# Attention and a two-matmul MoE block with Mish: three batches in one hand-ordered stream, one table set for Exp and Ln, Mish in one batched pass

## The chip, the cores and the metric

The kernel runs on one core of a Trainium2 chip. The metric is device time of one execution in microseconds (us), the median of several runs; shorter is better. A core has five engines that work side by side, each on its own queue: TensorE (PE, matmuls into PSUM, with weight loads called PEld), VectorE (DVE), ScalarE (ACT, activation functions from loaded tables), GpSimd (POOL) and SyncE (SP, here only a DMA queue).

## The reference, cut to what matters

```python
# q, k, v: (8 batches, 12 heads, 448 tokens, 64), scaled by 0.1
scores = (q @ k.T) / 8
m = max(scores); e = exp(scores - m)
attn = e / (sum(e) + exp(-m))          # softmax "off by one"
x = (attn @ v), heads side by side     # (3584 tokens, 768)
h = x @ w_in                           # 768 -> 2048
g = h * tanh(softplus(h))              # Mish
out = g @ w_out                        # 2048 -> 768
```

Without the maximum, the softmax is exp(s) / (sum(exp(s)) + 1), and both kernels compute it so: 1/(1+sum) is exp(-Ln(1+sum)).

## The kernel before

It works in two phases. All of attention comes first, two heads (a "pair") at a time, 48 pairs; the tokens' activations then stay in SBUF. The MoE phase follows in chunks of 512 tokens. The tile framework orders the instructions.

```python
# attention, for each of the two heads of a pair: four key tiles of 128 (the last padded)
for t in range(NSK):
    nc.tensor.matmul(sc_ps, lhsT=kT_bf[:, c0 + t*SKP : c0 + (t+1)*SKP], rhs=qT_bf, ...)  # zero-padded k
    nc.scalar.activation(out=eT_bf[:, t, :], in_=sc_ps, func=AF.Exp, scale=SCALE)        # L249
...                                       # av_ps: 64 rows of values, row 64 is the sum
nc.scalar.activation(out=dln[...], in_=av_ps[D:D+1, :], func=AF.Ln, bias=1.0)            # L277
nc.scalar.activation(out=rp[0:33, :], in_=dln, func=AF.Exp, scale=-1.0)                  # L127
nc.tensor.matmul(bc_ps, lhsT=blk_ones, rhs=rp, ...)     # spread the reciprocal over 64 rows
nc.vector.tensor_mul(xT_sb[...], av_keep[h_off][0:D, :], bc_sb[...])

# MoE, for each 128 x 512 tile of h (112 of them): Mish as h - h * 2/((1+e^h)^2 + 1)
nc.scalar.activation(out=u_sb, in_=h_ps, func=AF.Exp)                                    # L323
nc.scalar.activation(out=v_sb, in_=u_sb, func=AF.Square, bias=1.0)                       # L324
nc.scalar.activation(out=t_sb, in_=v_sb, func=AF.Ln, scale=0.5, bias=half_bias)          # L325
nc.scalar.activation(out=r_sb, in_=t_sb, func=AF.Exp, scale=-1.0)                        # L328
nc.vector.tensor_mul(p_sb, h_ps, r_sb)
nc.vector.tensor_sub(gT_bf[:, ff, :], h_ps, p_sb)
```

## Time and profile before

| | before |
|---|---|
| time, median | 1082.11 us (three runs; 1082.96 with a fourth) |
| ACT busy | 982.9 us of 1084.0 (91%) |
| PE busy (modelled) | 681.1 us (63%) |
| table loads on ACT | 341 of 1283 ns, 437 us |
| granted TensorE clock | 0.802 mean |

From the page of the kernel before: busy time of the engines, the granted clock of PE over 40 equal slices of the span (in tenths), and the engines' shares of the chain that ended last (a q marks an engine's sequencer).

```profile
PE 681.1 (63%) x2768; PEld 310.3 (29%) x2768; DVE 376.6 (35%) x962; ACT 982.9 (91%) x1345; POOL 60.4 (6%) x102
PEclk9766776778787766767877888888888888889889
ACT 62%; PE 21%; issue 13%; DVE 2%; DMA 1%; SPq 0%; ACTq 0%; POOL 0%; DVEq 0%
```

ACT is nearly always busy and holds most of the chain. What it is busy with is seen in its groups of instructions (line, engine, operation, count | busy us, mean ns of one | idle before):

```profile
L325 ACT ACT_TABLE_LOAD x112 | 143.7, 1283 | 2.0
L323 ACT ACT_TABLE_LOAD x81 | 103.9, 1283 | 1.4
L277 ACT ACT_TABLE_LOAD x58 | 74.4, 1283 | 1.0
L249 ACT ACT_TABLE_LOAD x46 | 59.0, 1283 | 15.2 <-DMA q_f_175<-in_q_dram 14.4
...
```

Exp and Ln alternate, and each change from one to the other is one load: in the MoE phase every Ln (L325, 112 tiles) and most of the Exps of L323 (81 of 112) need one. With 31 and 13 more before two further Exps, 341 in all, the loads take 44% of ACT's busy time (437 of 983 us) and compute nothing.

PE's own pace shows in two windows (start:end, length, then busy us and count of PE, PEld, DVE, ACT, POOL; PE clock, DMA share, GB/s). The first is ordinary MoE work, the second the last 34 us, where only the second matmul is left:

```profile
900.00:1000.00 100.00, 65.51 (x272) 29.58 (x272) 29.91 (x45) 98.77 (x123) 0.00 (x0) 0.86 0.06 23
1050.00:1084.00 34.00, 30.36 (x186) 18.06 (x184) 8.02 (x12) 12.71 (x20) 0.00 (x0) 0.98 0.18 70
```

With ACT out of the way PE gets a clock of 0.98. The timeline there has 16 matmuls of 512 columns plus 16 of 256 every 5.20 us: 12,288 columns, 2.36 per ns.

### The profile page before, as it was taken

The numbers are of one execution on the slowest core, as the hardware profiler recorded it, in microseconds if no ns is written. First come the engines' busy times: TensorE is split into PE (matmuls) and PEld (weight loads), VectorE is DVE, ScalarE is ACT, GpSimd is POOL, SyncE is SP. The second block draws the span as 40 slices with busy tenths as digits, with TensorE's granted clock in tenths as the row PEclk, the third lists the DMA queues.
The fourth block names the chain that finished last, engine by engine and source line by source line (L and its number), as shares of the span: only waits on it lengthen the run. The fifth ranks groups of instructions, "written<-read, shape, count | busy, mean of one in ns | idle before, by whom it ended". The sixth has DMA issues, their size and how long they took to land.

```text
span 1084.0 us, 9227 instructions
## 1 busy us (share of the span) xinstructions
PE 681.1 (63%) x2768; PEld 310.3 (29%) x2768; DVE 376.6 (35%) x962; ACT 982.9 (91%) x1345; POOL 60.4 (6%) x102
## 2 busy tenths in 40 slices
PE   3665666666666655656556656666677676676578
PEld 1322322332222222222222222232233232232235
DVE  5334443445444333322323323323223223223222
ACT  3888988888898889989999999999999999999992
POOL 2111111111111100000000000000000000000000
PEclk9766776778787766767877888888888888889889
DMA  9334444444433322200000000000000000000002
GB/s 241 90 78 111 111 120 119 108 104 118 106 77 77 74 54 58 48 1 1 0 1 29 0 30 0 15 15 29 15 15 30 15 15 30 15 15 29 15 15 88
DMA packets 143282, 57.24 MB, mean 53 GB/s; under 512 B 136064, under 2 KB 136064, under 8 KB 143232
## 3 DMA queue, kind: packets, MB, share of 16 engines
q1 hardware_dynamic: 139200, 44.07, 16.3%
q10 hardware_dynamic: 4032, 12.58, 3.7%
q8 instruction: 22, 0.36, 0.1%
q14 instruction: 28, 0.23, 0.1%
HBM read 45.61 MB, written 11.01 MB: 52 GB/s over the span
## 4 chain that ended last, share of the span: by engine, by line
ACT 62%; PE 21%; issue 13%; DVE 2%; DMA 1%; SPq 0%; ACTq 0%; POOL 0%; DVEq 0%
ACT L323 9%; PE sc_ps L242 9%; ACT t_sb L325 7%; PE av_ps L268 7%; ACT eT_bf L249 6%; ACT u_sb L323 6%; ACT L249 5%; ACT L277 5%; ACT v_sb L324 5%; ACT r_sb L328 5%; ACT L325 3%; ACT L328 3%; ACT dln_pair_71 L277 2%; ACT dln_pair_72 L277 2%; PE o_ps L340 2%
## 5 line engine op out<-in xcount | busy, mean ns | idle before, releaser
L311 PE MATMUL h_ps<-xT_sb,w_in_sb 128*128 128x512 bf16 x672 | 211.6, 464 | 202.5 <-DVE gT_bf L331 202.4
L249 ACT ACTIVATE eT_bf<-sc_ps 128x448 bf16<-128x448 f32 x384 | 200.0, 539 | 54.6 <-PE sc_ps L242 52.5
L329 DVE TENSOR_TENSOR p_sb<-h_ps,r_sb 128x512 f32<-128x512 f32 x112 | 77.5, 692 | 392.9 <-ACT r_sb L328 392.9
L268 PE MATMUL av_ps<-eT_bf,v_aug 128*65 128x448 bf16 x384 | 183.2, 495 | 17.6 <-ACT eT_bf L249 16.8
L311 PEld LDWEIGHTS <-w_in_sb 128*128 128x128 bf16 x672 | 74.4, 111 | 322.7 <-issue 278.2
L325 ACT ACT_TABLE_LOAD x112 | 143.7, 1283 | 2.0
L340 PE MATMUL o_ps<-w_out_sb,gT_bf 128*128 128x512 bf16 x448 | 134.7, 434 | 1.2 <-DVE o_sb L357 1.2
L242 PE MATMUL sc_ps<-qT_bf,kT_pad_75 128*128 128x448 bf16 x192 | 95.7, 502 | 60.7 <-ACT eT_bf L249 56.5
L242 PE MATMUL sc_ps<-qT_bf,kT_pad_76 128*128 128x448 bf16 x192 | 92.3, 482 | 64.5 <-ACT eT_bf L249 63.7
L268 PEld LDWEIGHTS <-v_aug 128*65 128x65 bf16 x384 | 59.2, 154 | 172.8 <-issue 166.7
L323 ACT ACT_TABLE_LOAD x81 | 103.9, 1283 | 1.4
L137 DVE CAST bc_sb<-bc_ps 128x448 bf16<-128x448 f32 x48 | 30.0, 625 | 186.1 <-PE bc_ps L135 182.6
L325 ACT ACTIVATE t_sb<-v_sb,half_bias 128x512 f32<-128x512 f32 x112 | 80.8, 722 | 1.3
L331 DVE TENSOR_TENSOR gT_bf<-h_ps,p_sb 128x512 bf16<-128x512 f32 x112 | 77.4, 691 | 4.0
L277 ACT ACT_TABLE_LOAD x58 | 74.4, 1283 | 1.0
L249 ACT ACT_TABLE_LOAD x46 | 59.0, 1283 | 15.2 <-DMA q_f_175<-in_q_dram 14.4
L328 ACT ACTIVATE r_sb<-t_sb 128x512 f32<-128x512 f32 x112 | 69.8, 624 | 0.3
L324 ACT ACTIVATE v_sb<-u_sb 128x512 f32<-128x512 f32 x112 | 69.5, 620 | 0.5
L348 PE MATMUL o_ps<-w_out_sb,gT_bf 128*128 128x256 bf16 x448 | 69.7, 296 | 0.0
L340 PEld LDWEIGHTS <-gT_bf 128*128 128x128 bf16 x448 | 49.9, 111 | 68.7 <-issue 33.2
L323 ACT ACTIVATE u_sb<-h_ps 128x512 f32<-128x512 f32 x112 | 66.5, 593 | 0.9
L141 DVE TENSOR_TENSOR xT_sb<-av_ps,bc_sb 64x448 bf16<-64x448 f32 x96 | 59.1, 616 | 5.2
(331 smaller groups left out, 590.6 us busy)
## 6 DMA issues: line engine op xcount, KB each, us to landing
out_dram<-o_sb SPq DMA_DIRECT2D x28, 384.0 KB, 2.3
stage<-in_moe_w_in_dram ACTq DMA_DIRECT2D x12, 512.0 KB, 4.5
stage<-in_moe_w_out_dram ACTq DMA_DIRECT2D x16, 384.0 KB, 3.2
q_f_108<-in_q_dram SPq DMA_DIRECT2D x2, 112.0 KB, 6.1
k_f_109<-in_k_dram SPq DMA_DIRECT2D x2, 112.0 KB, 6.6
q_f_175<-in_q_dram SPq DMA_DIRECT2D x2, 112.0 KB, 4.9
k_f_176<-in_k_dram SPq DMA_DIRECT2D x2, 112.0 KB, 5.6
q_f_261<-in_q_dram SPq DMA_DIRECT2D x2, 112.0 KB, 4.0
```

Source lines behind the costliest of these rows:

```text
L242: nc.tensor.matmul(sc_ps, lhsT=kT_bf[:, c0 + t * SKP : c0 + (t + 1) * SKP], rhs=qT_bf, start=True, stop=True,)
L249: nc.scalar.activation(out=eT_bf[:, t, :], in_=sc_ps, func=AF.Exp, scale=SCALE)
L268: nc.tensor.matmul(av_ps, lhsT=v_augs[h_off][:, t, :], rhs=eT_bfs[h_off][:, t, :], start=(t == 0), stop=(t == NSK - 1),)
L277: nc.scalar.activation(out=dln[h_off * 32 : h_off * 32 + 1, :], in_=av_ps[D : D + 1, :], func=AF.Ln, bias=1.0,)
L311: nc.tensor.matmul(h_ps, lhsT=w_in_sb[:, dm, ff * 128 : (ff + 1) * 128], rhs=xT_sb[:, dm, t0 : t0 + TOK_CHUNK], start=(dm == 0), stop=(dm ...
L323: nc.scalar.activation(out=u_sb, in_=h_ps, func=AF.Exp)
L324: nc.scalar.activation(out=v_sb, in_=u_sb, func=AF.Square, bias=1.0)
L325: nc.scalar.activation(out=t_sb, in_=v_sb, func=AF.Ln, scale=0.5, bias=half_bias)
L328: nc.scalar.activation(out=r_sb, in_=t_sb, func=AF.Exp, scale=-1.0)
L329: nc.vector.tensor_mul(p_sb, h_ps, r_sb)
L331: nc.vector.tensor_sub(gT_bf[:, ff, :], h_ps, p_sb)
L340: nc.tensor.matmul(o1_ps, lhsT=gT_bf[:, ff, ts * 128 : (ts + 1) * 128], rhs=w_out_sb[:, ff, 0:N1], start=(ff == 0), stop=(ff == FF_T - 1),)
```

## The change

The intent: take ACT off the critical path and keep PE busy without a break.

- One table set that holds Exp and Ln is loaded by hand; Mish is one table pass, run in a batch for 16 tiles at once.
- Attention of batch p, the first matmul of batch p-1 and the second matmul of batch p-2 run in one stream whose order is written by hand. A slot is one head pair plus a few "units" of MoE work (one h tile, or half of one output tile).
- Keys are cut into 384 (three tiles of 128) plus a tail of 64. The score matmuls of the two heads use the two 64-row halves of PE side by side, and so do the tails of attention times v.
- 64 ones columns stand beside v, so the sum of a head arrives in 64 rows at once; the matmul that spread the reciprocal is gone.
- The weights are cast to bf16 by the DMA itself, issued by GpSimd.

The diff, cut to its core (some lines joined, comments added):

```diff
-        sc_ps, lhsT=kT_bf[:, c0 + t * SKP : c0 + (t + 1) * SKP], rhs=qT_bf,      # 8 a pair
-        nc.scalar.activation(out=eT_bf[:, t, :], in_=sc_ps, func=AF.Exp, scale=SCALE)
+            for h in range(2):
+                r = slice(h * D, h * D + D)
+                nc.tensor.matmul(sp[:, h, 0:S], lhsT=qk[r, S + t * 128 : S + (t + 1) * 128],
+                                 rhs=qk[r, 0:S], start=True, stop=True)
+            nc.scalar.activation(out=e[:, 2 * t : 2 * t + 2, :], in_=sp[:, :, 0:S], func=AF.Exp, ...)
 [...]
+            nc.scalar.activation(out=ln[r, :], in_=av[h][o, 0:S], func=AF.Ln, bias=1.0)
+        nc.scalar.activation(out=rc, in_=ln, func=AF.Exp, scale=-1.0)
 [...]
-                nc.scalar.activation(out=u_sb, in_=h_ps, func=AF.Exp)
-                nc.scalar.activation(out=v_sb, in_=u_sb, func=AF.Square, bias=1.0)
-                nc.scalar.activation(out=t_sb, in_=v_sb, func=AF.Ln, scale=0.5, bias=half_bias)
-                nc.scalar.activation(out=r_sb, in_=t_sb, func=AF.Exp, scale=-1.0)
-                nc.vector.tensor_mul(p_sb, h_ps, r_sb)
-                    nc.vector.tensor_sub(gT_bf[:, ff, :], h_ps, p_sb)
+    def mish(b):
+        for i in range(4):
+            nc.scalar.activation(out=gm[:, f, :], in_=h_sb[:, f, 0:MAIN], func=AF.Mish)
+        nc.scalar.activation(out=gt[:, :, o : o + TAIL], in_=h_sb[:, :, MAIN:S], func=AF.Mish)
+        nc.scalar.preload_act_table_set("natural_log_exp_and_others")
 [...]
+        def slot(j, units):
+            if j + 3 < J: load(j + 3)
+            if j + 2 < J: do_cast(j + 2)
+            rest = max(0, len(units) - 2)
+            scores(j, 0); take(1); transposes(j + 1); take(1)
+            attend(j - 1); scores(j, 1); take((rest + 1) // 2)
+            normalize(j - 1); take(len(units))
+        for p in range(B):
+            m1 = mm1_units(p - 1) if p >= 1 else []
+            m2 = mm2_units(p - 2) if p >= 2 else []
+            for i in range(NPAIR):           # slot 0: 4 of m2; slots 1 to 4: 4 of m1; slot 5: rest of m2
+                ...
+                if i == 4 and p >= 1:
+                    mish(p - 1)              # under it: 8 units of m2
```

## The prediction

> **What bounds the kernel now.** ScalarE (ACT). The page gives it 982.9 us of the 1084.0 us span; VectorE 376.6, TensorE (PE) 681.1 of modelled busy time. The chain that ended last is 62% ACT. The groups of instructions show why: 341 ACT_TABLE_LOADs of 1283 ns, 437 us in all, because Exp and Ln alternate. In the MoE stage (from about 496 us) each 128x512 tile costs four ACT passes (593, 620, 722, 624 ns) and two loads: ACT is 98-99% busy there, 86-90% in attention.
>
> PE is starved: in the windows from 50 to 1050 us its granted clock is 0.67 to 0.86. Only the last 34 us, pure second matmul, run at 0.98: there 16 matmuls of 512 columns plus 16 of 256 take 5.20 us, 2.36 columns per ns.
>
> **What the change does to ACT.** The table set with both Exp and Ln is loaded by hand, so loads fall to about 17 (22 us). The Trainium skill ("ScalarE: Activation LUTs", Table sets) says that one set holds both; this trace shows no such set in use. Per head pair, 8 Exps of 448 (539 ns, about 460 back to back) become three of 896 (about 0.91 us) and one of 448, plus two Ln and one Exp of 448: 4.8 us, 230 us in all. Mish becomes one pass from SBUF, about 7 us a batch. ACT total: about 310 us (estimate from the durations above). It leaves the critical path.
>
> **VectorE:** transpose copies, two 64x448 multiplies a pair (616 ns), 112 h copies (about 0.6 us), 56 output copies: about 200 us, not binding.
>
> **PE becomes the bound.** Columns streamed: mm1 344,064, mm2 344,064, scores 150,528, attention times v 172,032, transposes 43,008: 1,053,696, or 446 us at 2.36 columns per ns. If the K=64 score pairs and the v tails, in different row halves, run concurrently, 86,000 columns vanish: 409 us. The skill ("TensorEngine Tiling (Array Packing)", Key Properties) says that changing the tiling mode drains PE, so I count half of that gain.
>
> **Sum by stage** (estimates):
> - start and batch 0, attention alone, competing with 12.6 MB of weights: 60 us
> - batch 1: 52 us, its Mish (10 us with two loads) covered by no second matmul
> - six steady batches: 51-56 us of PE plus 2-4 us of waits, 56 each: 336 us
> - last attention, mm1 of batch 7 with direct Mish, mm2 of batches 6 and 7, last store: 67 us
>
> Predicted: 515 us, 475 to 565 for 8 in 10. Faster by over 2%: 0.98; same 0.01; slower 0.01.
>
> **What would show it.** Right: about 17 table loads; ACT below 65% of the span; PE clock above 0.93 from about 60 us on; PE busy above 85%; chain mostly PE; steady period about 56 us. The score matmuls of a pair start within tens of ns of each other if they run concurrently, about 190 ns apart if not. Wrong: ACT still over 80% (loads inserted anyway, or slow Mish passes); clock still at 0.8 in the dense part (then 600 us or more); PE idle at the PSUM pools of two buffers (transposes and av share one), over 1 us a slot; the first matmul of batch 1 waiting for w_in beyond 70 us.
>
> **What would make it wrong.** Weight casts in the DMA issued by GpSimd may arrive late or be starved; a stall per slot of 1 us is worth 48 us; the in-order ACT queue may put one pair's Ln behind another's Exps.

## The result, and the profile after

The changed kernel takes 548.13 us (544.7 to 548.82) against 1082.96, and gives a correct result. The ratio is 0.5052, 95% interval 0.5032 to 0.5071. Ratios here are the mean time of one kernel's fast runs over that of the other's in the same rounds, so they differ a little from the ratio of the quoted medians. A second set of runs, the control of the last experiments, gave 547.44 us:

> The changed kernel unchanged, as the control beside the three that follow on the same chip: 548 us within 3, ratio to the kernel before 0.503 to 0.507.

From the page of the changed kernel, the same three lines:

```profile
PE 483.3 (88%) x2768; PEld 234.0 (43%) x2768; DVE 206.3 (38%) x414; ACT 297.9 (55%) x419; POOL 130.2 (24%) x400
PEclk9999869986999899999999899999999999989999
PE 82%; ACT 6%; DMA 6%; SPq 3%; DVE 1%; issue 1%; POOL 0%; POOLq 0%
```

ACT has fallen from 91% to 55% of a span half as long, and the chain is now PE. Of the table loads, 16 are left (these 14, one at the start and one at the Mish of the last batch), from its groups of instructions:

```profile
L233 ACT ACT_TABLE_LOAD x7 | 9.0, 1283 | 0.1
L235 ACT ACT_TABLE_LOAD x7 | 9.0, 1283 | 0.1
L233 ACT ACTIVATE gm<-h_sb 128x1536 bf16<-128x1536 f32 x28 | 39.2, 1470 | 0.1
```

Mish runs at one table pass's price: 1536 columns in 1.47 us. The span cut by stage, with the boundaries at the first score matmul of slots 6 and 12 and at the last pair's attention (windows, columns as above):

```profile
0.00:70.70 70.70, 34.84 (x138) 11.16 (x139) 15.21 (x37) 27.01 (x40) 31.28 (x91) 0.95 0.85 186
70.70:126.50 55.80, 43.97 (x234) 18.85 (x234) 22.77 (x47) 36.88 (x51) 15.47 (x49) 0.84 0.28 76
126.50:481.50 355.00, 346.32 (x2069) 171.73 (x2068) 158.59 (x315) 221.34 (x295) 83.45 (x260) 0.98 0.30 85
481.50:546.40 64.90, 58.17 (x329) 32.22 (x327) 9.72 (x18) 12.67 (x37) 0.00 (x0) 0.96 0.14 49
```

| stage | predicted | measured |
|---|---|---|
| start and batch 0 | 60 | 70.7 |
| batch 1 | 52 | 55.8 |
| six steady batches | 336 (56 each) | 355.0 (59.2 each) |
| last attention and MoE tail | 67 | 64.9 |

(The records of the clock begin at 60.2 us and read 1.00 before that, so the 0.95 of the first line is too high: the matmuls of batch 0 run at half speed, as experiment 10 shows.) The first and the third stage hold nearly all of the surplus. For the third, here is one steady slot of PE (timeline: start us, duration, engine, line, operation, operands, count):

```profile
255.81 0.55 PE L149 MATMUL s_ps<-qk 64*128 64x448 bf16 x4
256.29 1.31 PE L205 MATMUL h_ps<-xT,w_in_sb 128*128 128x448 bf16 x6
257.44 0.33 PE L125 MATMUL tr_ps<-ident,qmb 128*128 128x128 bf16 x3
257.70 0.20 PE L129 MATMUL tr_ps<-ident,qtb 64*128 64x64 bf16 x1
257.83 0.34 PE L125 MATMUL tr_ps<-ident,kmb 128*128 128x128 bf16 x3
258.11 0.20 PE L129 MATMUL tr_ps<-ident,ktb 64*128 64x64 bf16 x1
258.24 1.31 PE L205 MATMUL h_ps<-xT,w_in_sb 128*128 128x448 bf16 x6
259.39 1.30 PE L172 MATMUL av_ps<-e,v_aug_84 128*128 128x448 bf16 x6
260.62 0.36 PE L181 MATMUL av_ps<-e,v_aug_84 64*128 64x448 bf16 x2
260.82 0.35 PE L149 MATMUL s_ps<-qk 64*128 64x448 bf16 x2
261.10 0.36 PE L161 MATMUL s_ps<-qk,k_tail_94 128*128 128x448 bf16 x1
261.30 2.43 PE L205 MATMUL h_ps<-xT,w_in_sb 128*128 128x448 bf16 x12
```

Two things are to be read from the start times. First, the two halves do run concurrently: two 64-row matmuls of 448 columns are over in 0.20 us (260.62 to 260.82), the time of one. The single records say it more finely: the second of such a pair starts a median of 4 ns after the first (144 pairs of score matmuls, 99% of them under 10 ns). Second, wherever 64-row and 128-row matmuls follow each other, time is missing. Six 448-column matmuls need 1.14 us at 189 ns each (the spacing of the records); the six at 259.39 need 1.23 before the next may start. The records show 285 ns in place of 189 at such a place, 96 ns more, and 0.80 us for transposes whose 896 columns are worth 0.38. A slot has eight such changes (two around the first scores, four at the transposes, two around the tails), so some 0.77 us; the slot's columns are 16,576, or 7.0 us, and it lasts 7.9 to 8.0.

The start shows in the timeline of GpSimd, which issues the weight loads and also makes the casts of q, k and v:

```profile
11.66 3.34 POOL L287 DMA_DIRECT2D w_in_sb<-in_moe_w_in_dram  x6
14.94 1.55 POOL L293 DMA_DIRECT2D w_out_sb<-in_moe_w_out_dram  x2
18.11 0.74 POOL L293 DMA_DIRECT2D w_out_sb<-in_moe_w_out_dram  x1 [1.61 <-DMA w_in_sb<-in_moe_w_in_dram]
20.90 0.74 POOL L293 DMA_DIRECT2D w_out_sb<-in_moe_w_out_dram  x1 [2.04 <-DMA w_in_sb<-in_moe_w_in_dram]
21.68 0.50 POOL L102 CAST qmb<-qm 128x384 bf16<-128x384 f32 x1
...
34.82 0.51 POOL L102 CAST kmb<-km 128x384 bf16<-128x384 f32 x1 [2.47 <-DMA km<-in_k_dram]
```

From 11.66 to 21.68 us GpSimd does nothing but issue weights, the last two waiting for earlier ones to land. The casts for the third pair come only then, and those after it wait for q and k, which share the DMA engines with the weights. The trace has this too: the loads of q before the weights land 2.5 to 2.7 us after their issue, the next two, issued at 14.6 and 25.0 us, after 15.7 and 17.4. Slots 0 to 6 start at 6.5, 12.0, 29.7, 42.7, 54.4, 62.7 and 70.8 us.

### The profile page after: what moved, and what is told of

The parts are those of the page before. It is cut to its first block, busy times and chain, and to the rows that moved or that the text cites. A ratio compares the mean times of both kernels' runs of the same rounds, so it can differ in the third digit from the quotient of the medians.

```text
span 546.4 us, 7802 instructions
## 1 busy us (share of the span) xinstructions
PE 483.3 (88%) x2768; PEld 234.0 (43%) x2768; DVE 206.3 (38%) x414; ACT 297.9 (55%) x419; POOL 130.2 (24%) x400
## 4 chain that ended last, share of the span: by engine, by line
PE 82%; ACT 6%; DMA 6%; SPq 3%; DVE 1%; issue 1%; POOL 0%; POOLq 0%
PE o_ps L248 28%; PE h_ps L205 28%; PE av_ps L172 10%; PE s_ps L149 6%; PE tr_ps L125 4%; DMA km<-in_k_dram 3%; PE av_ps L181 3%; DMA kt<-in_k_dram 2%; PE tr_ps L129 2%; PE s_ps L161 2%; ACT e L156 2%; ACT ln L189 1%; ACT rc L190 1%; SPq L78 1%; ACT gm L233 1%
## 5 line engine op out<-in xcount | busy, mean ns | idle before, releaser
L205 PE MATMUL h_ps<-xT,w_in_sb 128*128 128x448 bf16 x768 | 164.7, 358 | 2.0 <-DVE xT L200 2.0
L189 ACT ACTIVATE ln<-av_ps 64x448 f32<-64x448 f32 x96 | 51.7, 539 | 172.9 <-PE av_ps L181 171.7
L156 ACT ACTIVATE e<-s_ps 128x896 bf16<-128x896 f32 x144 | 126.0, 909 | 22.5 <-PE s_ps L149 20.1
L248 PE MATMUL o_ps<-w_out_sb,gm 128*128 128x384 bf16 x768 | 134.9, 333 | 0.0
L213 DVE COPY h_sb<-h_ps 128x448 f32<-128x448 f32 x112 | 70.0, 625 | 97.0 <-PE h_ps L205 96.1
L248 PEld LDWEIGHTS <-gm 128*128 128x128 bf16 x768 | 75.3, 99 | 53.0 <-issue 5.1
L200 DVE TENSOR_TENSOR xT<-av_ps,rc 64x448 bf16<-64x448 f32 x96 | 59.7, 622 | 74.9 <-ACT rc L190 72.6
L149 PE MATMUL s_ps<-qk 64*128 64x448 bf16 x288 | 52.8, 384 | 27.1 <-ACT e L156 26.1
L256 DVE COPY o_sb<-o_ps 128x384 f32<-128x384 f32 x56 | 31.2, 557 | 100.1 <-PE o_ps L248 99.5
L233 ACT ACTIVATE gm<-h_sb 128x1536 bf16<-128x1536 f32 x28 | 39.2, 1470 | 0.1
```

The lines of the kernel that those rows point to most:

```text
L149: nc.tensor.matmul(sp[:, h, 0:S], lhsT=qk[r, S + t * 128 : S + (t + 1) * 128], rhs=qk[r, 0:S], start=True, stop=True,)
L156: nc.scalar.activation(out=e[:, 2 * t : 2 * t + 2, :], in_=sp[:, :, 0:S], func=AF.Exp, scale=SCALE)
L189: nc.scalar.activation(out=ln[r, :], in_=av[h][o, 0:S], func=AF.Ln, bias=1.0)
L200: nc.vector.tensor_mul(x_t[b][r, hp, :], av[h][r, 0:S], rc[r, :])
L205: nc.tensor.matmul(hp[:, 0:S], lhsT=w_in_sb[:, dm, ff * 128 : (ff + 1) * 128], rhs=x_t[b][:, dm, :], start=(dm == 0), stop=(dm == DM_T - 1),)
L213: nc.vector.tensor_copy(out=h_sb[:, ff, :], in_=hp[:, 0:S])
```

## The experiments

Theory: the old kernel was bound by table loads on ACT; the new one by PE, which loses its surplus over the predicted columns in three places: the start (weights in the way), changes between 64-row and 128-row matmuls, and slots without MoE work, where PE waits and then often gets half its clock. The rivals stand in each expectation. Times are medians; the kernel before, run beside them, took 1083.8 to 1084.94. The runs were made in three calls on three chips (1 to 4; 5, 6, 7 and 9; 8 and 10), and the changed kernel ran again only in the last, so the ratios compare best across calls.

### 1. Only the hand-loaded table set, in the old kernel

```diff
+    nc.scalar.preload_act_table_set("natural_log_exp_and_others")
     singles = ctx.enter_context(tc.tile_pool(name="singles", bufs=1))
```

> The kernel before with one line added: the table set that holds Exp and Ln is loaded by hand at the start, nothing else changed. Theory A (table switches alone bound the old kernel): 341 loads of 1283 ns fall to a handful, ACT busy falls from 983 to about 550 us, the old structure then runs at its next limits (MoE near PE, attention near ACT), total 600 to 680 us, correct result. Theory B (the old kernel was bound by its chain of Exp, Square, Ln, Exp and by tile order, not by the loads): 850 us or more. Theory C (loads are inserted all the same): 1080 us and 341 loads again.

Measured: 615.59 us (ratio 0.569, interval 0.566 to 0.572), correct, and exactly one table load where there had been 341. From its page, the engines and the granted clock:

```profile
PE 529.8 (87%) x2768; PEld 257.3 (42%) x2768; DVE 376.5 (62%) x962; ACT 524.4 (86%) x1005; POOL 60.2 (10%) x102
PEclk9998989999999999999999999999999999999999
ACT 41%; PE 33%; DMA 11%; issue 7%; DVE 5%; SPq 2%; POOL 1%; ACTq 0%; POOLq 0%; DVEq 0%
```

Theory A holds. One line takes 469 us off, more than the 437 us of the loads themselves. In the two traces ACT's busy time falls by 458 us: 436 are loads, and 22 come from passes that now overlap, as no load stands between them. ACT's idle time falls by another 14. PE's clock rises from 0.80 to 0.99; whether it has a part in the 14 was not tested. So 87% of the 537 us that the whole change gains can be had in the old structure by this line.

### 2. The table set and the table Mish, still in two phases

```diff
-    [four ACT passes and two VectorE operations of a tile]
+                nc.scalar.activation(out=gT_bf[:, ff, :], in_=h_ps, func=AF.Mish)
```

> As the run before it, and in the MoE stage the four ACT passes and two VectorE operations of a tile are replaced by one Mish table pass from PSUM. Batches are not pipelined: attention first, then MoE. If the pipelined stream of the change is what brings it near 548 us, this stays 40 us or more above it (attention about 290 us bound by ACT, MoE about 300 us bound by PE: 590). If the two table edits carry nearly everything, it comes within 20 us of 548.

Measured: 596.62 us (0.5507), correct. ACT busy falls from 524 to 343 us and the time by only 19: the MoE phase was by then near PE's bound (in experiment 1, from 400 to 500 us, PE is busy for 98.78 us and ACT for 84.04). What remains to the changed kernel is 49 us. In the window from 100 to 200 us ACT is busy for 96.05 us of 100 and PE for 81.22; from 400 to 500 us PE for 100.00 and ACT for 27.93. Each phase has one engine full and another with slack. That is what the stream of three batches is meant to remove: it lays the ACT work of attention beside the PE work of MoE. No run takes the stream alone, though: the 49 us also hold the packed matmuls, the matmul that is gone and the other start, so what the stream by itself is worth is not shown.

### 3. The changed kernel without the hand loads

```diff
-        nc.scalar.preload_act_table_set("natural_log_exp_and_others")   # both places
```

> The changed kernel without the two hand loads of a table set; loads go where the compiler puts them. Theory A (ACT has slack in the pipelined stream): about 96 more loads in the slots, ACT busy from 298 to about 420 us, time up by 10 to 60 us. Theory B (ACT is near the critical chain of each slot): up by 100 us or more, the full 123 us of loads.

Measured: 601.99 us (0.5551), 112 loads, ACT busy 420.8 us: 54 us slower, at the top of theory A. From its groups:

```profile
L189 ACT ACT_TABLE_LOAD x48 | 61.6, 1283 | 0.8
L190 ACT ACT_TABLE_LOAD x48 | 61.6, 1283 | 0.8
```

Two loads a slot, 2.57 us, make a slot last 9.3 us in place of 8.0. More than half of the 123 us is hidden in ACT's slack. The rest is not: PE's waits for the exponentials (the score matmuls, for PSUM that an Exp has yet to read) rise from 26.1 to 71.3 us. The same edit is worth 469 us in the old kernel and 54 us here.

### 4. Mish tile by tile instead of in one pass

```diff
-            nc.vector.tensor_copy(out=h_sb[:, ff, :], in_=hp[:, 0:S])
[...]
         nc.scalar.activation(out=gm[:, ff, :], in_=hp[:, 0:MAIN], func=AF.Mish)      # now in all batches
         nc.scalar.activation(out=gt[:, ff, o : o + TAIL], in_=hp[:, MAIN:S], func=AF.Mish)
+        if b < B - 1:
+            nc.scalar.preload_act_table_set("natural_log_exp_and_others")
[...]
+            m1 = mm1_units(p - 1, direct=True) if p >= 1 else []
```

> The changed kernel with Mish taken tile by tile straight from PSUM in every batch (as it does for the last one), with a table load before and after each tile; the batched pass and the h copy are gone. Theory: batching is needed because of the loads: up to 2 loads for each of 112 tiles, some 290 us more on ACT, ACT becomes the bound and the time rises to 700 us or more. Rival: PE slack hides most of it: below 620 us.

Measured: 789.45 us (0.728, two runs), 226 loads, ACT 58% of the chain. Batching Mish is not a refinement: with the table in another set than Exp, it is what makes the table Mish usable inside an attention stream.

### 5. One full transpose for both tails

The tails of q and k are put into the two halves of one 128-row tile and transposed by one full matmul.

```diff
-                tail = stage.tile([64, 2, D], FP32, ...)              # one for q, one for k
+                    qkt = stage.tile([128, 2, D], FP32, ...)          # q in rows 0-63, k in 64-127
...
-            nc.tensor.transpose(ps[:, c : c + TAIL], tb..., ident[0:64, 0:64])      # for q and for k
+            nc.tensor.transpose(ps[:, c0 : c0 + 128], got["t"]..., ident)           # once
```

> The changed kernel with the 64-row tails of q and k cast into one 128-row tile and transposed by one full matmul, in place of two 64-row transposes: four changes between 64-row and 128-row matmuls a slot are gone. Theory (each such change costs PE about 0.1 us): the transposes of a slot fall from 0.80 to about 0.40 us, 13 to 19 us in all, time about 530 us. Rival (the gaps are the transposes' own cost or are hidden): within 4 us of 548.

Measured: 529.43 us (0.488, interval 0.487 to 0.489), 18 us less. PE at the same place of a slot, from its timeline:

```profile
257.99 0.33 PE L133 MATMUL tr_ps<-ident,qmb 128*128 128x128 bf16 x3
258.16 0.22 PE L127 MATMUL tr_ps<-ident,tb 128*128 128x128 bf16 x1
258.21 0.33 PE L133 MATMUL tr_ps<-ident,kmb 128*128 128x128 bf16 x3
258.38 1.30 PE L209 MATMUL h_ps<-xT,w_in_sb 128*128 128x448 bf16 x6
```

The transposes take 0.39 us (257.99 to 258.38) in place of 0.80, with the same number of columns. Steady slots fall from 8.0 to 7.6 us; 48 slots times 0.41 would be 20. The cost of the changes of mode is shown, not only argued. The edit also drops one small matmul and one cast a slot, but experiment 6 shows the same cost without them: the twelve matmuls before unpacked scores take 2.27 us there (259.48 to 261.75), and 2.37 in the changed kernel before packed ones (261.30 to 263.67).

### 6. Score matmuls on all 128 rows

```diff
-                    lhsT=qk[r, S + t * 128 : ...], rhs=qk[r, 0:S],
+                    lhsT=qk[:, S + t * 128 : ...], rhs=qk[:, 0:S],
```

> Wrong result on purpose: the score matmuls of a pair use all 128 rows (as a zero-padded k would, the cost is the same), so the two of a pair run one after the other, and no change of tiling mode surrounds the first two pairs. Theory (packing two heads into the row halves is a net gain of 0.56 us less 0.2 us of mode changes a slot): 10 to 20 us slower than 548. Rival (the mode changes eat the gain): within 4 us, or faster.

Measured: 550.25 us (0.5077, interval 0.5053 to 0.510) against 548.13 and 547.44: no clear difference, so the rival's number came out. Its timeline shows why in two lines of one slot:

```profile
261.75 0.92 PE L148 MATMUL s_ps<-qk 128*128 128x448 bf16 x4
262.50 1.30 PE L204 MATMUL h_ps<-xT,w_in_sb 128*128 128x448 bf16 x6
```

Four score matmuls now take 0.75 us, against 0.48 with packing (255.81 to 256.29). A steady slot lasts 8.2 us in place of 7.9 to 8.0, so packing is still a gain of 0.2 to 0.3 us there, half of the 0.56 us that its columns suggest. But batches 0 and 1 together are 5.1 us shorter without packing (slot 12 starts at 121.4 us, not 126.5): PE, with more to do, drops to half clock less often. Slots 4 to 6 take 6.7 us at full clock there, in place of 8.0 to 8.3 at half clock:

```profile
61.40 0.97 PE L148 MATMUL s_ps<-qk 128*128 128x448 bf16 x4 [1.92 <-ACT e L155]
64.08 1.12 PE L171 MATMUL av_ps<-e,v_aug 128*128 128x448 bf16 x5 [0.70 <-DVE k_tail L137]
```

(The changed kernel's five attention matmuls take 2.05 us there, at 65.63.) In these two traces 6.6 us are given back between the starts of slots 12 and 47, so the two nearly cancel. Neither theory was quite right: the mode changes take part of the gain, the clock the rest (seen in one trace of each).

The scores are wrong. With q and k scaled by 0.1 the scores have a standard deviation of 0.01, attention is close to uniform, and even exactly uniform attention would be 1% off in norm. The comparison cannot see the scores. So each winning edit (5, 7, 8, 9 and 10) was also run in a simulation of values with q and k ten times larger and v three times, and Silu in place of Mish, which the simulation lacks: their outputs differ from a float computation by 0.47% in norm, as does the changed kernel's; this experiment's differs by 119%.

### 7. The weights one piece a slot, and 8. only w_out late

```diff
-        for dm in range(DM_T): nc.gpsimd.dma_start(out=w_in_sb[:, dm, :], ...)   # all before slot 0
-        for i in range(4):     nc.gpsimd.dma_start(out=w_out_sb[...], ...)
+            if j < DM_T: load_w_in(j)                    # in slot j; left at the start in experiment 8
+            elif j < DM_T + 4: load_w_out(j - DM_T)
```

> The changed kernel with the MoE weights fetched one piece a slot (w_in in slots 0 to 5, w_out in 6 to 9) in place of all ten pieces at once before slot 0. Theory (the 12.6 MB of weights crowd out the loads of q, k and v, and GpSimd, which issues them, cannot cast meanwhile): slot 6 starts at 56 to 62 us in place of 70.8, time down 9 to 15 us. Rival (attention alone is bound by its own chain at a cold clock, about 8.3 us a slot, and the first matmul of batch 1 waits for w_in): within 4 us of 548.

> The changed kernel with w_in issued at once as before, and only w_out fetched late (slots 6 to 9). It parts two causes of the slow start. Theory A (GpSimd stuck in the issue of w_out until 21.7 us is what holds up slot 2): slot 2 starts 7 to 10 us earlier than its 29.7 us, and most of the 19 us that the piecewise load of all weights won is won here too. Theory B (the share of the DMA engines that w_in takes is the cause): slot 2 is earlier, but slots 3 and 4 stay late, and less than half of the 19 us is won.

Measured: 528.82 us (0.4878) with all weights by pieces, 540.07 us (0.4978) with only w_out late. Slot 2 starts at 20.9 and 23.9 us in place of 29.7, slot 6 at 53.9 and 64.4 in place of 70.8. Against the control (0.5038), w_out alone gives 6.5 us (0.6% of 1084.5), a third of the 19. So theory B of experiment 8 holds for the larger part: slot 3 stays late (40.0 us, where 42.7 was and experiment 7 has 29.2), held up by the shared DMA engines while w_in lands (the load of q issued at 14.7 us lands at 30.6, as late as in the changed kernel, and the last piece of w_in lands at 31.8); GpSimd stuck in the issue of w_out is the smaller part. The parting is not clean, as a GpSimd that is free earlier also asks for its loads earlier. In experiment 7 the gain was larger than forecast (19 us, not 9 to 15). What stays from slot 1 on is 8.0 to 9.0 us a slot.

### 9. MoE units spread otherwise

```diff
-                    units, m2 = m2[:4], m2[4:]
+                    n0 = 4 if len(m2) > 12 else 2        # even batches: 2 in slot 0, 2 in slot 5
...
-        slot(J, [])
+        slot(J, m2[:4])
```

> The changed kernel with the units of the second matmul spread otherwise: in even batches 2 units in slot 0 and 2 in slot 5 (before: 4 and 0), and 4 units in the last slot (before: none). Theory (a slot without units lets PE idle about 3 us and drops its clock): the dips to half clock near 184, 305, 425 and 480 us go away, 8 to 16 us less. Rival (the idle time only moves to slot 0): within 4 us of 548.

Measured: 537.29 us (0.4952, interval 0.4941 to 0.4963), 11 us less. The steady spells of half clock are gone: in the changed kernel the records have them at 186, 306 and 487 us; here there is none between 132 us and the last 2 us. (The dip that the expectation names at 425 us is not in the records: PE waits 2.1 us at 422.8 as it does at 186.1 and 304.5, and keeps its clock.) The rival is out: the idle time did not merely move.

### 10. All three together, and useless matmuls

```diff
+            if idle:                       # a slot without MoE units
+                warm(3)                    # after the transposes: 3 matmuls into a PSUM tile nobody reads
 ...
+                warm(6)                    # after the last score matmul
```

> All three edits that won alone, together: one transpose for both tails, weights one piece a slot, units spread. If their gains (18.7, 19.3 and 10.8 us) lie in different places they add up: 499 us, 495 to 507. If they overlap: above 510.

> The one before it, with nine useless matmuls of 448 columns in each slot that has no MoE work (three after the transposes, six after the last score matmul), which nothing reads. Theory (in batch 0 PE is too idle to be granted its full clock, and its cold matmuls lengthen the chain of a slot: 8.3 us a slot, 6.7 with the busier full-row scores): slots of batch 0 fall to 6.5 to 7 us, 8 to 12 us less in all. Rival (the chain of exponentials sets the slot, or the extra matmuls delay real ones): no gain, or slower.

Measured: 503.70 us (0.4645, interval 0.4636 to 0.4654) for the three edits together, 4.4 us short of the plain sum of 48.8 us. With the useless matmuls 493.56 us (0.4553, interval 0.4542 to 0.4564), correct: 10 us more. The first is PE in a slot of batch 0 of the combined kernel:

```profile
29.05 0.99 PE L153 MATMUL s_ps<-qk 64*128 64x448 bf16 x4 [1.73 <-ACT e L160]
...
31.93 2.05 PE L176 MATMUL av_ps<-e,v_aug 128*128 128x448 bf16 x5 [0.66 <-DVE k_tail L141]
...
37.06 0.99 PE L153 MATMUL s_ps<-qk 64*128 64x448 bf16 x4 [1.74 <-ACT e L160]
```

And the same slot with the useless matmuls, of which `warm_ps` is the output:

```profile
28.18 0.80 PE L153 MATMUL s_ps<-qk 64*128 64x448 bf16 x4 [0.98 <-ACT e L160]
29.32 0.73 PE L323 MATMUL warm_ps<-qk,ident 128*128 128x448 bf16 x3
30.51 1.12 PE L176 MATMUL av_ps<-e,v_aug 128*128 128x448 bf16 x5 [0.28 <-DVE k_tail L141]
32.25 1.30 PE L323 MATMUL warm_ps<-qk,ident 128*128 128x448 bf16 x6
34.53 0.80 PE L153 MATMUL s_ps<-qk 64*128 64x448 bf16 x4 [0.98 <-ACT e L160]
```

Five attention matmuls fall from 2.05 to 1.12 us: the clock has doubled. The slot falls from 8.0 to 6.35 us although PE does nine matmuls more. PE was never idle for more than 1.74 us at a time there, and yet stayed at half clock. The idle time alone does not tell when: the slots of experiment 6 that keep the full clock have a gap of 1.92 us and are idle for 39% of their time, these for 30%. What they have more of is work, 7,168 columns in 6.7 us against 5,824 in 8.0 (packed pairs counted once). This is the fastest version: 9.8% less than the changed kernel (493.56 against 547.44), 54% less than the kernel before.

## Why the prediction was right or wrong

The time, 548 us, lies in the range of 475 to 565, 6% above the point of 515. Point by point:

- **ACT is the bound, by its table loads, and leaves the critical path: right.** The loads were forecast at 17 and are 16; ACT at 310 us and is 297.9; PE holds 82% of the chain. Experiment 1 shows the cause by itself. The Trainium skill's page "ScalarE: Activation LUTs", section "Table sets: the hidden batching unit", says that one set holds Exp and Ln; one load in experiment 1 agrees.
- **Fewer loads alone: not asked, and the largest lesson.** The prediction treated the change as one. 469 of its 537 us come from one line that needs none of the restructuring.
- **PE columns at 2.36 per ns: right.** The records are 189 ns apart for 448 columns, 2.37 per ns.
- **"I count half of that gain" (row packing): right in size, by luck, wrong in form.** The half was a guess without a working. Pairs run fully concurrently, 4 ns apart, so the columns do vanish. What is paid is 96 ns for each change between 64 and 128 rows: the four around the scores and v tails come to 18 us of the 36 that the columns are worth, and so to half. "TensorEngine Tiling (Array Packing)", section "Key Properties", says that a change drains PE; the 96 ns agree with it. The prediction looked only at the scores and the v tails; four of the eight changes sit at the transposes, which gain nothing from it (experiment 5).
- **"six steady batches: 51-56 us of PE plus 2-4 us of waits, 56 each": mis-sized by 3.2 us a batch, 19 in all.** It measured 59.2. Of this, 51.2 is columns with packing (120,960 a batch on average), about 4.6 the changes of mode (eight in each of six slots, 96 ns), 1.4 the waits for ACT and VectorE within that window (8.5 us in six batches, less than the 2 to 4 a batch predicted), and the rest, about 2.0, spells of half clock and small gaps. The last is a remainder, not a measurement; the records have half clock for 12 us of the window, which by estimate costs 6, or 1.0 a batch. So the term that was too small is PE's own time, by the mode changes above all.
- **"start and batch 0: 60 us": mis-sized by 10.7 us.** The risk was named (weight casts by GpSimd), not its size. With the weights by pieces (experiment 7) the stage ends at 53.9, so issuing all weights first costs 17 us of it. The prediction also held the clock to be above 0.93 "from about 60 us on"; it is 0.84 over batch 1, and experiment 10 shows that batch 0 runs at half clock as well.
- **"batch 1: 52 us": 55.8.** PE waits 6.5 us for ACT there, under the Mish that nothing covers, as forecast.
- **Two-buffer PSUM pools: no stall of over 1 us a slot on average.** The waits for a buffer in the steady window are the 8.5 us above, 0.24 a slot; three of the 36 slots wait 2.1.

## What to carry to other kernels

Before restructuring, count the table loads of ACT and ask for one set that serves all functions of a loop; alone, here, this took 43% off the time. When PE is the bound, count the changes between 64-row and 128-row matmuls as well as the columns: packing halves loses part of its gain to them (half, here), and a small odd-sized matmul between full ones can cost more than its work. Where PE waits for another engine again and again, it can stay at half clock, and matmuls that nobody reads can buy the clock back; look at the spacing of the matmuls, as neither the longest gap nor the idle share told it here.

## What the Trainium skill lacked or had wrong

- "TensorEngine Tiling (Array Packing)", "Key Properties", names the drain at a change of tiling mode but gives no size. Here a change between 64-row and 128-row matmuls costs 96 ns (285 in place of 189 ns between starts), and taking four of eight out of each slot wins 18 us of 548.
- "TensorE: Matmul & The Clock Gate", section "Why this matters for your kernels", asks for no idle gap of more than about 3 us between bursts of matmuls. In the slots of batch 0 that experiment 10 shows the gaps are at most 1.74 us and the matmuls still run at half clock (2.05 us for five, 1.12 with the useless ones added). The idle share does not decide either: in experiment 6 slots with a gap of 1.92 us and 39% idle time, against 30%, keep full clock. What orders the three cases is the work: 5,824 columns in 8.0 us at half clock, 7,168 in 6.7 and 9,856 in 6.35 (with the useless matmuls) at full clock. No run seeks the threshold, or parts the number of columns from the rows in use.
- The same page, section "Back-to-back issue gap", gives 131 ns a matmul at 512 columns for a sustained stream with weight loads. Here 448 columns with a weight load each are 189 ns apart, and the old kernel's 512 columns 216 (sixteen in 3.45 us), which is its "isolated" formula.
- "ScalarE: Activation LUTs", section "What ACT_TABLE_LOAD costs", puts a switch at about 2.66 us, of which about 1.38 is a drain. The loads here take the page's 1283 ns, the ACTIVATE before ends at 113.02 us, the load starts at 113.04 and the next ACTIVATE at 114.33: no further 1.38 us is seen.
- No page says how the granted clock in a trace reads before the first change is recorded: in the changed kernel's trace the first 60 us show 1.00 while matmuls run at half speed (five of 448 columns in 2.05 us at 24.59 and at 57.59). There the spacing of matmuls is the better witness.
